# Attention and a gated product on one core: four blocks of the first product placed ahead of their Mish, one transposition by DMA, loads in another order

## The chip, the core and the metric

The kernel runs on one core of a Trainium2 chip. The core has a matrix engine (TensorE, PE in the profile; its weight loads are PEld), a vector engine (VectorE, DVE), an engine for activation functions (ScalarE, ACT), a general engine (GpSimd, POOL) and SyncE (SP), which here only issues DMA transfers. Each engine works through a queue of its own in order; semaphores join them. Matrix products go to PSUM, and VectorE or ScalarE bring them from there to SBUF. The metric is the device time of one execution in microseconds (us).

## The reference

Attention with one more term in the denominator, for 8 batches of 12 heads, 448 rows and 64 columns, and then two products with Mish between them:

```python
scores = scale * np.matmul(q, k.transpose(0, 1, 3, 2))
m = np.max(scores, axis=-1, keepdims=True)
e = np.exp(scores - m)
attn = e / (np.sum(e, axis=-1, keepdims=True) + np.exp(-m) + 1e-09)
out = np.matmul(attn, v)
...
x = out.transpose(0, 2, 1, 3).reshape(3584, 768)
h = x @ w_in                      # 768 x 2048
g = h * np.tanh(softplus(h))      # Mish
y = g @ w_out                     # 2048 x 768
```

## The kernel before

**Pairs, steps and units.** Two heads make a pair: 6 pairs per batch, 48 in all. A pair's 7 blocks of 128 score rows are handled in 4 steps, the first three with two blocks, the last with one. For each step TensorE makes the scores in one of three double PSUM tiles (`sc`), VectorE takes the negated row maximum (L293), ScalarE the exp with its sum (L306). Scores run up to three steps ahead (`scores_ahead`, L239), since a score tile is free once its exp is done.

Batch 0 (pairs 0 to 5) runs alone at the start, the head (loop at L548). Then come units of three pairs, that is 12 steps (loop at L575, `u` from 2; `n` counts steps). A unit's steps are followed by a block: the first product of half a batch (8 blocks of 128 hidden columns, 6 matmuls each, `mm1_mish`, L399), one Mish by ScalarE for each. Unit 2 and 3 hold batch 1's pairs and batch 0's first product, 4 and 5 batch 2's pairs and batch 1's first product, and so on. ScalarE loads a table when it goes from exp to Mish and another when it goes back (L649).

**Second product.** From unit 4 on, pieces of the second product fill TensorE's time between steps (`plan`, L490 and on; `mm2_part`, L443): a part is 16 matmuls for 128 rows and half of the columns (384). Unit 4 has 2.5 parts and unit 5 has 3.5, dealt out by `weight`, about a third of them at step 0.

**Normalisation, transposition, output.** After a unit's last exp the block normalises its pairs (`normalise`, L325): two by VectorE, one by GpSimd (`on_pool`), which takes a copy of the reciprocals (`rden2`) first. In the head GpSimd does four of a pair's seven blocks (`shared`). Each normalised pair has to be transposed for the output product: by a DMA that SP issues (L345), or, for the pairs in `BY_PE` (2, 4, 5, 6, 7), by four turns of TensorE of seven transposes each (L356) with a copy by VectorE (L360). `todo` (L625) sorts the unit's pairs so that those of `BY_PE` come last. `av_pair` (L368) makes the output product into a tile `mo` (there are two) and a copy `xT` (L391); from unit 4 on the output of the last unit's pair goes into the free half of the fourth step's score tile (`av_with`, L260). Copies out of `mo` are put into `late` and issued at the next `flush_late`.

**Loads.** Each pair's q, k and v (224 KB each) come by three DMAs on SP's queue, into four buffers each; GpSimd casts them to bf16 (`cast_pair`). In units this is done at steps 0, 3 and 6 (`LOAD_AT`), the load for four pairs on, the cast for three. The weights come in 20 pieces by GpSimd's queue, in order: 12 of `w_in` (256 KB, three for each quarter of its columns), 8 of `w_out` (384 KB, four for each half of its columns).

**Zeros and middle rows.** From pair 12 on, two of three pairs have their queries laid out with zero blocks (`is_diag`) so that both heads share one matmul; VectorE clears these tiles at pairs 13 and 14 (L223, L224). 448 rows are three and a half blocks of 128, so the half block of two batches is gathered in `mid` (`gather_mid`, L416).

The order of the work is written out by hand; the tables that the change touches are these:

```python
BY_PE = (2, 4, HEAD - 1, HEAD, HEAD + 1)          # HEAD = 6
AV_AT = ({3: 4, 7: 3, 9: 5}, {5: 6, 8: 7, 10: 8})   # step: pair, units 2 and 3
W_AT = ({5: 1, 9: 1}, {1: 1, 4: 1, 5: 1, 7: 1, 9: 1, 11: 1}, {3: 1, 5: 1, 7: 1, 9: 1})
```

Of the kernel before, what the change touches and what calls it, by code (L numbers as in the profile page):

```python
# [19 lines left out]
def kernel(  # L20
# [9 lines left out]
    nc = tc.nc  # L30
# [170 lines left out]
    def evac_qk(p, act=False):  # L201
        if p >= N_PAIRS:
            return
        (q_ps, k_ps), own = qkT[p]
        mo_free.extend(own)
        qd = q_diag[p % 3]
        kT = qk_pool.tile([128, S], BF16, tag="kT", name="kT")
        if not is_diag(p):
            qT = qd.rearrange("d i h r -> d (i h r)")[:, 0:S]
            qkT[p] = (qT, kT)  # L210
            if act:
                nc.scalar.mul(qT, q_ps[:, 0:S], SCALE)
            else:
                nc.vector.tensor_scalar(
                    out=qT, in0=q_ps[:, 0:S], scalar1=SCALE, scalar2=None, op0=ALU.mult
                )
            if p >= DIAG_FROM:
                nc.gpsimd.tensor_copy(out=q_rest[0:64, 0, :], in_=qT[0:64, 384:S])
                nc.gpsimd.tensor_copy(out=q_rest[64:128, 1, :], in_=qT[64:128, 0:64])
        else:  # L220
            qkT[p] = (qd, kT)
            if p < DIAG_FROM + 3:
                nc.vector.memset(qd[0:64, :, 1, :], 0.0)  # L223
                nc.vector.memset(qd[64:128, :, 0, :], 0.0)  # L224
# [100 lines left out]
    def normalise(p, dma=True, on_pool=False, shared=0):  # L325
        st = att[p]
        en = st["en"]
        if on_pool or shared:
# [3 lines left out]
        for i in range(NTILE):  # L332
# [63 lines left out]
        del att[p], casted[p], qkT[p]  # L396


    def mm1_mish(b, ff):  # L399
        if ff == 0:  # L400
            gT[b] = gT_pool.tile([128, FF_T, S], BF16, tag="gT", name="gT")
        flush_late()
        spare = ff % FF_U == 1
        h_ps = sc_tiles[0][:, 0, :] if spare else mo_take()
        for dm in range(DM_T):
            nc.tensor.matmul(  # L406
                h_ps[:, 0:S],
                lhsT=w_in_sb[:, dm, ff * 128 : (ff + 1) * 128],
                rhs=xT[b][:, dm, :],
                start=(dm == 0), stop=(dm == DM_T - 1),  # L410
            )
        nc.scalar.activation(out=gT[b][:, ff, :], in_=h_ps[:, 0:S], func=AF.Mish)  # L412
        if not spare:
            mo_free.append(h_ps)

    def gather_mid(b):  # L416
# [5 lines left out]
        nc.vector.tensor_copy(  # L422
            out=mids[g][:, :, 64 * half : 64 * half + 64], in_=gT[b][:, :, at : at + 64]
        )

# [67 lines left out]
    for g in range(B // 2):  # L493
        u0 = first_mm2 + 4 * g
        rest = plan.pop(u0, [])
        if g == 0:
            plan[u0] = [(0, i, 0, 2) for i in range(2)] + [(0, 2, 0, 1)]
            plan[u0 + 1] = [(0, 2, 1, 1)] + [(0, i, 2, 2) for i in range(3)]
        else:
            plan[u0] = rest + whole(g, 0) + [(g, 1, 0, 1)]  # L500
            plan[u0 + 1] = [(g, 1, 1, 1), (g, 1, 2, 2)] + whole(g, 2)
# [4 lines left out]
        else:  # L506
# [5 lines left out]
    BY_POOL = 4  # L512
    LEAD = UNIT_PAIRS + 1
    LOAD_AT = (0, 3, 6)
    LAST_AV_AT = (0, 6, 9)
    HEAD = HP

    BY_PE = (2, 4, HEAD - 1, HEAD, HEAD + 1)
    TURN_AT = (
        {0: [(4, 2)], 1: [(4, 3)], **{3 + j: [(HEAD - 1, j)] for j in range(NT)}},  # L520
        {0: [(HEAD, 0), (HEAD, 1)], 1: [(HEAD, 2)], 2: [(HEAD, 3)],
         3: [(HEAD + 1, 0)], 4: [(HEAD + 1, 1)], 5: [(HEAD + 1, 2)], 6: [(HEAD + 1, 3)]},
    )
    TURN_HEAD = {
        (3, 2): [(2, 0)], (3, 3): [(2, 1)], (4, 0): [(2, 2)], (4, 1): [(2, 3)],
# [49 lines left out]
    for u in range(UNITS_PER_B, N_UNITS + 2 * UNITS_PER_B):  # L575
# [3 lines left out]
            filler.extend(mm2_part(*part))  # L579
        total, done, acc = sum(w for _, w in filler), 0, 0.0  # L580
        p0 = u * UNIT_PAIRS
        if attn and u >= first_mm2:
            av_with.update({p0 + i: p0 + i - UNIT_PAIRS for i in range(UNIT_PAIRS)})
        end = min((u + 1) * UNIT_PAIRS, N_PAIRS) * STEPS

        for n in range(steps):
# [18 lines left out]
            scores_ahead(end)  # L605
            if n in LOAD_AT:
                load_pair(p0 + LOAD_AT.index(n) + LEAD)
                cast_pair(p0 + LOAD_AT.index(n) + LEAD - 1)
            if u - UNITS_PER_B < len(AV_AT):
                early = AV_AT[u - UNITS_PER_B]  # L610
                if n in early:
                    av_pair(early[n])
                if u == UNITS_PER_B:
# [33 lines left out]
        if attn and u + 1 < N_UNITS:  # L647

            nc.scalar.activation(out=one, in_=zero, func=AF.Exp)  # L649
        if moe and w == UNITS_PER_B - 1:  # L650
            gather_mid(b)
    flush_late()
    assert not pieces and all(have == 4 for _, have in o_sbs.values())
# [30 lines left out]
```

## Time and profile before

| | us |
|---|---|
| median of three runs | 480.3 (480.15 to 481.88) |
| the profiled execution | 479.95 |
| its span, first to last instruction | 478.0 |
| TensorE busy in it | 443.1 (93%) |
| ScalarE busy | 350.0 (73%) |
| VectorE busy | 339.1 (71%) |
| GpSimd busy | 181.1 (38%) |

The first exp of unit 3 starts at 76.75, that of unit 4 at 104.29, of unit 5 at 130.17, of unit 6 at 156.91. A line of the page names a place in the code (L406), an engine, an operation, and tiles (`gT<-mo`). A digit in a row of 40 is a busy share in tenths. Start-to-start times are the ones to use for matmuls, since one begins while the last still runs: an L406 block of six takes 1.14 us, a matmul of 384 columns at L472 0.163 us. The granted clock of TensorE is 1.00 or 0.50 in stretches of 3.41 us; it was 0.50 at 44.5 to 54.8, 78.7 to 82.1 and 88.9 to 92.3 of the span.

### The profile page before, as it was taken

What the parts mean: (1) busy time and instruction counts of PE and PEld (TensorE: products, weight loads), DVE (VectorE), ACT (ScalarE), POOL (GpSimd) and SP (SyncE); (2) the same over time, 40 slices, a digit from 0 to 9 for tenths busy, and PEclk for the clock granted to TensorE, in tenths of its full rate; (3) what the DMA queues carried; (4) which work ended last, traced back from release to release, by engine and by line L of the source; (5) the groups of instructions that cost most, each with busy time, mean ns of one, the idle gap of its engine ahead of it and who ended that gap; (6) DMA issues with size and microseconds to landing.
All of it is one profiled execution on the core that took longest, in us unless ns stands there. A gap on an engine that the chain in (4) does not pass through costs nothing.

```text
span 478.0 us, 8924 instructions
## 1 busy us (share of the span) xinstructions
PE 443.1 (93%) x3064; PEld 248.6 (52%) x3064; DVE 339.1 (71%) x680; ACT 350.0 (73%) x919; POOL 181.1 (38%) x315
## 2 busy tenths in 40 slices
PE   4565888898999999999999999999999999999997
PEld 2233544454655555555555555556555555556565
DVE  4888987968787886878687878788787869420021
ACT  5979678878787888979787878888897978412300
POOL 4877809255514334353535242433535340300000
PEclk9998798899999999999999999999999999999999
DMA  8999969999999989899999999899989595870113
GB/s 228 220 233 220 235 100 234 162 187 238 207 217 276 206 212 219 213 203 246 193 250 182 225 167 228 211 207 234 201 233 212 156 178 127 135 164 24 43 28 105
DMA packets 202381, 90.37 MB, mean 189 GB/s; under 512 B 159072, under 2 KB 198880, under 8 KB 202336
## 3 DMA queue, kind: packets, MB, share of 16 engines
q1 hardware_dynamic: 194848, 83.51, 81.3%
q0 software_dynamic: 7488, 6.29, 8.6%
q8 instruction: 24, 0.39, 0.3%
q14 instruction: 21, 0.17, 0.1%
HBM read 45.61 MB, written 11.01 MB: 118 GB/s over the span
## 4 chain that ended last, share of the span: by engine, by line
PE 76%; ACT 10%; DVE 9%; issue 2%; DMA 1%; POOL 0%; SPq 0%; DVEq 0%; ACTq 0%; POOLq 0%
PE mo L472 26%; PE mo L406 25%; ACT en L306 9%; PE sc L382 6%; DVE negm L293 6%; PE sc L266 5%; PE sc L406 4%; PE sc L193 3%; PE sc L272 2%; PE mo L356 1%; PE mo L382 1%; DVE en L341 1%; PE sc L280 1%; DVE eT L360 1%; DMA k_f<-in_k_dram 1%
## 5 line engine op out<-in xcount | busy, mean ns | idle before, releaser
L306 ACT ACTIVATE en<-sc,negm 128x448 bf16<-128x448 f32 x336 | 209.6, 637 | 26.4 <-DVE xT L391 10.4
L293 DVE TENSOR_REDUCE negm<-sc 128x2 f32<-128x896 f32 x192 | 180.7, 968 | 55.8 <-PE sc L275 26.0
L472 PE MATMUL mo<-w_out_sb,gT 128*128 128x384 bf16 (+1 forms) x912 | 142.3, 301 | 0.0
L406 PE MATMUL mo<-xT,w_in_sb 128*128 128x448 bf16 x672 | 137.7, 353 | 0.6 <-DVE xT L391 0.6
L412 ACT ACTIVATE gT<-mo 128x448 bf16<-128x448 f32 x112 | 61.3, 547 | 68.2 <-PE mo L406 68.1
L472 PEld LDWEIGHTS <-gT 128*128 128x128 bf16 x912 | 84.1, 98 | 48.2 <-issue 5.7
L339 POOL TENSOR_SCALAR en<-en,rden 128x448 bf16<-128x448 bf16 x122 | 76.4, 646 | 80.7 <-DVE rden L331 76.9
L406 PEld LDWEIGHTS <-w_in_sb 128*128 128x128 bf16 x768 | 72.9, 98 | 64.0 <-issue 3.0
L306 ACT ACTIVATION_READ_ACCUMULATOR en<-sc,negm 128x1 f32 x336 | 69.3, 206 | 0.0
L175 POOL CAST q_bf<-q_f 112x512 bf16<-112x512 f32 x47 | 29.0, 617 | 98.4 <-DMA q_f<-in_q_dram 98.0
L341 DVE TENSOR_SCALAR en<-en,rden 128x448 bf16<-128x448 bf16 x214 | 58.6, 345 | 0.9
L459 DVE COPY o_sb<-mo 128x384 f32<-128x384 f32 (+1 forms) x65 | 32.2, 495 | 35.1 <-PE mo L472 34.8
L266 PE MATMUL sc<-kT,qd 128*128 128x448 bf16 x168 | 47.7, 354 | 0.3 <-ACT en L306 0.2
L272 PE MATMUL sc<-kT,qd 64*128 64x448 bf16 x72 | 25.1, 411 | 12.7 <-ACT en L306 11.1
L382 PE MATMUL sc<-eT,v_bf 112*64 112x448 bf16 x288 | 34.1, 357 | 1.9 <-ACT en L306 1.7
L162 POOL CAST v_bf<-v_f 112x512 bf16<-112x512 f32 x48 | 29.5, 616 | 9.7 <-DMA v_f<-in_v_dram 8.8
L382 PEld LDWEIGHTS <-v_bf 112*64 112x64 bf16 x384 | 21.0, 112 | 22.8 <-issue 13.6
L176 POOL CAST k_bf<-k_f 112x512 bf16<-112x512 f32 x47 | 28.9, 616 | 7.5 <-DMA k_f<-in_k_dram 7.0
L227 DVE TENSOR_SCALAR qd<-sc 64x448 bf16<-64x448 bf16 x48 | 18.7, 389 | 11.9 <-PE sc L193 11.2
L266 PEld LDWEIGHTS <-qd 128*128 128x128 bf16 x168 | 16.3, 97 | 18.0 <-issue 9.2
L275 PE MATMUL sc<-kT,qd 64*128 64x448 bf16 x72 | 25.4, 415 | 0.0
L472 PE MATMUL mo<-w_out_sb,mid 128*128 128x384 bf16 x128 | 24.9, 326 | 0.0
(57 smaller groups left out, 340.1 us busy)
## 6 DMA issues: line engine op xcount, KB each, us to landing
q_f<-in_q_dram SPq DMA_DIRECT2D x48, 224.0 KB, 5.1
k_f<-in_k_dram SPq DMA_DIRECT2D x48, 224.0 KB, 5.4
v_f<-in_v_dram SPq DMA_DIRECT2D x48, 224.0 KB, 5.7
w_in_sb<-in_moe_w_in_dram POOLq DMA_DIRECT2D x12, 256.0 KB, 6.1
w_out_sb<-in_moe_w_out_dram POOLq DMA_DIRECT2D x8, 384.0 KB, 7.6
out_dram<-o_sb SPq DMA_DIRECT2D x7, 336.0 KB, 3.3
out_dram<-o_sb SPq DMA_DIRECT2D x8, 288.0 KB, 4.6
out_dram<-o_sb SPq DMA_DIRECT2D x8, 240.0 KB, 2.9
```

Of the source, the lines that this page charges most:

```text
L162: nc.gpsimd.tensor_copy(out=casted[p][2], in_=loaded.pop(p)[2])
L266: nc.tensor.matmul(sc[:, bk, 0:S], lhsT=qT[:, i].rearrange("d h r -> d (h r)"), rhs=kT, start=True, stop=True,)
L272: nc.tensor.matmul(sc[:, 0, 0:S], lhsT=qT[0:64, qa : qa + 128], rhs=kA, start=True, stop=True)
L293: nc.vector.tensor_reduce(out=negm, in_=sc[:, 0 : len(cols), 0:S], axis=AX.X, op=ALU.max, negate=True)
L306: nc.scalar.activation(out=st["en"][:, :, c, 0:SP_], in_=sc[:, bk, 0:S].rearrange("q (j c) -> q j c", j=NT), func=AF.Exp, bias=st["negm"][ ...
L339: nc.gpsimd.tensor_scalar(scalar2=1.0, op0=ALU.mult, op1=ALU.mult, **args)
L341: nc.vector.tensor_scalar(scalar2=None, op0=ALU.mult, **args)
L382: nc.tensor.matmul(av[h * 64 : (h + 1) * 64, 0:S], lhsT=v_bf[:, h, j * D : (j + 1) * D], rhs=e_h, start=(j == 0), stop=(j == NT - 1),)
L406: nc.tensor.matmul(h_ps[:, 0:S], lhsT=w_in_sb[:, dm, ff * 128 : (ff + 1) * 128], rhs=xT[b][:, dm, :], start=(dm == 0), stop=(dm == DM_T - 1),)
L412: nc.scalar.activation(out=gT[b][:, ff, :], in_=h_ps[:, 0:S], func=AF.Mish)
L459: nc.vector.tensor_copy(out=o_sb[:, cols], in_=st["o"][:, 0:n_cols])
L472: nc.tensor.matmul(st["o"][:, 0:n_cols], lhsT=src[:, ff, c0 : c0 + 128], rhs=w_out_sb[:, ff, cols], start=(ff == 0), stop=(ff == FF_T - 1),)
```

## The change

- **First product ahead.** In unit 3, four of batch 0's blocks (8 to 11) are multiplied at steps 5, 7, 9 and 10, each into an `mo` tile, and copied by VectorE to an `o_sb` buffer in float32. In the block their Mish reads that buffer. Blocks 12 to 15 stay in the block; the two kinds alternate (`SECOND`). The block that uses a score tile (`spare`) is now the second of each unit's list.
- **Seventh pair.** Pair 6 leaves `BY_PE`; unit 2 normalises 6, 8 (VectorE), 7 (GpSimd), and two DMA transpositions are issued there. Pair 7's turns on TensorE are at steps 1 to 4 of unit 3; the outputs of pairs 6, 7, 8 at steps 3, 6, 8.
- **Loads.** Pairs 13 and 14 are loaded in unit 2 (step 9, block), 15, 16 and 17 in unit 3 (steps 0 and 10, block), 18 in unit 4's block. Casts stay where they are.
- **Weights.** In unit 2's block two pieces are issued at its third place instead of one each at the third and seventh; unit 3 issues its six by step 9 instead of 11; unit 4 three at steps 4 and 5 and the last in its block, instead of four up to step 9.
- **Unit 4 and 5.** Outputs of pairs 9, 10, 11 are made at steps 3, 7, 10 of unit 4 into `mo` tiles; `av_with` starts with unit 5. The second product has 3 parts in each of the two units.
- **GpSimd.** It clears the zero blocks once, ahead of unit 3's block, and gathers batch 0's half block at step 8 of unit 5.
- **Head.** For pairs 0 and 1 VectorE's three normalisations come ahead of the `rden2` copy and GpSimd's four.

```diff
-            if p < DIAG_FROM + 3:
-                nc.vector.memset(qd[0:64, :, 1, :], 0.0)
-                nc.vector.memset(qd[64:128, :, 0, :], 0.0)
...
+        order = list(range(NTILE))
+        if shared and p < 2:
+            order = order[shared:] + order[:shared]
+        for i in order:
+            if i == 0 and (on_pool or shared):
+                for_pool()
...
+    def mm1_ahead(b, ff):
+        h_ps = mo_take()
+        mm1(b, ff, h_ps)
+        h_sb = o_pool.tile([128, d_model], FP32, tag="o_sb", name="o_sb")
+        h_sbs[b, ff] = h_sb
+        def evac():
+            nc.vector.tensor_copy(out=h_sb[:, 0:S], in_=h_ps[:, 0:S])
+            mo_free.append(h_ps)
+        late.append(evac)
+
+    def mm1_mish(b, ff, spare):
...
+        if (b, ff) in h_sbs:
+            nc.scalar.activation(out=gT[b][:, ff, :], in_=h_sbs.pop((b, ff))[:, 0:S], func=AF.Mish)
+            return
...
-            plan[u0] = [(0, i, 0, 2) for i in range(2)] + [(0, 2, 0, 1)]
-            plan[u0 + 1] = [(0, 2, 1, 1)] + [(0, i, 2, 2) for i in range(3)]
+            plan[u0] = [(0, i, 0, 2) for i in range(3)]
+            plan[u0 + 1] = [(0, i, 2, 2) for i in range(3)]
...
+    W_MISH = {(2, 2): 2, (4, 1): 1}
+    LOADS = {
+        2: ({0: 10, 3: 11, 6: 12, 9: 13}, {1: 14}),
+        3: ({0: 15, 10: 16}, {4: 17}),
+        4: ({}, {1: 18}),
+    }
...
-    BY_PE = (2, 4, HEAD - 1, HEAD, HEAD + 1)
+    BY_PE = (2, 4, HEAD - 1, HEAD + 1)
     TURN_AT = (
...
-        {0: [(HEAD, 0), (HEAD, 1)], 1: [(HEAD, 2)], 2: [(HEAD, 3)],
-         3: [(HEAD + 1, 0)], 4: [(HEAD + 1, 1)], 5: [(HEAD + 1, 2)], 6: [(HEAD + 1, 3)]},
+        {1 + j: [(HEAD + 1, j)] for j in range(NT)},
...
-    AV_AT = ({3: 4, 7: 3, 9: 5}, {5: 6, 8: 7, 10: 8})
-
-    W_AT = ({5: 1, 9: 1}, {1: 1, 4: 1, 5: 1, 7: 1, 9: 1, 11: 1}, {3: 1, 5: 1, 7: 1, 9: 1})
+    AV_AT = ({3: 4, 7: 3, 9: 5}, {3: 6, 6: 7, 8: 8}, {3: 9, 7: 10, 10: 11})
+    FIRST_AT = {5: FF_U, 7: FF_U + 1, 9: FF_U + 2, 10: FF_U + 3}
+    SECOND = [ff for i in range(4) for ff in (FF_U + i, FF_U + 4 + i)]
+
+    W_AT = ({5: 1, 9: 1}, {1: 1, 2: 1, 4: 1, 5: 1, 7: 1, 9: 1}, {4: 2, 5: 1})
...
-        if attn and u >= first_mm2:
+        if attn and u > first_mm2:
...
+            if (u, n) == (first_mm2 + 1, 8):
+                gather_mid(0, nc.gpsimd.tensor_copy)
...
+        if u == UNITS_PER_B + 1:
+            for t_ in q_diag[1:]:
+                nc.gpsimd.memset(t_[0:64, :, 1, :], 0.0)
+                nc.gpsimd.memset(t_[64:128, :, 0, :], 0.0)
...
-                mm1_mish(b, w * FF_U + f)
-            if u == UNITS_PER_B and f in (2, 6):
-                load_w(1)
+                mm1_mish(b, SECOND[f] if u == UNITS_PER_B + 1 else w * FF_U + f, spare=f == 1)
```

More of the change, by code (lines that the diff above doesn't have):

```diff
@@ L327, in normalise, with for_pool @@
         en = st["en"]
-        if on_pool or shared:
+        def for_pool():
             st["rden2"] = st_pool.tile([128, NTILE], FP32, tag="rden2", name="rden2")
             nc.vector.tensor_copy(out=st["rden2"], in_=st["rden"])
-        for i in range(NTILE):
+        order = list(range(NTILE))
[4 more added lines that the diff above has]
+                for_pool()
             pool_does = on_pool or i < shared
@@ L396, in av_pair, with mm1 @@
         del att[p], casted[p], qkT[p]
[L399 to L404, printed above, removed]
+    def mm1(b, ff, h_ps):
         for dm in range(DM_T):
@@ L411, in mm1_mish @@
             )
+    h_sbs = {}
+    def mm1_ahead(b, ff):
[8 more added lines that the diff above has]
+    def mm1_mish(b, ff, spare):
+        if ff == 0:
+            gT[b] = gT_pool.tile([128, FF_T, S], BF16, tag="gT", name="gT")
+        flush_late()
+        if (b, ff) in h_sbs:
+            nc.scalar.activation(out=gT[b][:, ff, :], in_=h_sbs.pop((b, ff))[:, 0:S], func=AF.Mish)
+            return
+        h_ps = sc_tiles[0][:, 0, :] if spare else mo_take()
+        mm1(b, ff, h_ps)
         nc.scalar.activation(out=gT[b][:, ff, :], in_=h_ps[:, 0:S], func=AF.Mish)
@@ L414, in mm1_mish, with gather_mid @@
             mo_free.append(h_ps)
-    def gather_mid(b):
+    def gather_mid(b, copy=nc.vector.tensor_copy):
         g, half = divmod(b, 2)
@@ L421, in gather_mid @@
         at = S - 64 if half == 0 else 0
-        nc.vector.tensor_copy(
+        copy(
             out=mids[g][:, :, 64 * half : 64 * half + 64], in_=gT[b][:, :, at : at + 64]
@@ L605 @@
             scores_ahead(end)
+            if u in LOADS:
+                if n in LOADS[u][0]:
+                    load_pair(LOADS[u][0][n])
+            elif n in LOAD_AT:
+                load_pair(p0 + LOAD_AT.index(n) + LEAD)
             if n in LOAD_AT:
-                load_pair(p0 + LOAD_AT.index(n) + LEAD)
                 cast_pair(p0 + LOAD_AT.index(n) + LEAD - 1)
@@ L612 @@
                     av_pair(early[n])
+                if u == UNITS_PER_B + 1 and n in FIRST_AT:
+                    mm1_ahead(0, FIRST_AT[n])
                 if u == UNITS_PER_B:
@@ L627 @@
             if moe:
-                mm1_mish(b, w * FF_U + f)
-            if u == UNITS_PER_B and f in (2, 6):
-                load_w(1)
+                mm1_mish(b, SECOND[f] if u == UNITS_PER_B + 1 else w * FF_U + f, spare=f == 1)
+            if (u, f) in W_MISH:
+                load_w(W_MISH[u, f])
+            if u in LOADS and f in LOADS[u][1]:
+                load_pair(LOADS[u][1][f])
             if not attn:
@@ L649 @@
             nc.scalar.activation(out=one, in_=zero, func=AF.Exp)
-        if moe and w == UNITS_PER_B - 1:
+        if moe and w == UNITS_PER_B - 1 and b > 0:
             gather_mid(b)
```

## The prediction

> **What bounds the kernel now.** I read first the 40 slices of the page, to see where TensorE stops being the bound.
>
> ```profile
> PE   4565888898999999999999999999999999999997
> ...
> ACT  5979678878787888979787878888897978412300
> ...
> PEclk9998798899999999999999999999999999999999
> ```
>
> From the eleventh slice (119.5 us) on TensorE is full nearly to the end, so work taken off it there, or moved ahead of there, is worth its length; before, it has holes. The table by stretches shows the holes. I cut at ScalarE's first and last exp of units 2 to 5, so the rows alternate between steps and product block.
>
> ```profile
> 76.75:91.90 15.15, 11.62 (x86) 6.71 (x86) 12.97 (x19) 13.44 (x43) 9.94 (x16) 0.79 1.16 208
> 91.90:104.30 12.40, 12.40 (x87) 6.75 (x86) 8.98 (x29) 8.60 (x18) 4.65 (x9) 0.98 0.90 160
> 104.30:119.30 15.00, 13.07 (x89) 7.22 (x88) 12.76 (x18) 13.56 (x44) 7.83 (x14) 1.00 1.08 228
> ...
> 130.20:145.30 15.10, 15.08 (x96) 7.85 (x95) 12.50 (x18) 13.62 (x43) 3.70 (x7) 1.00 1.05 228
> ```
>
> Columns: length, then busy time of PE, PEld, DVE, ACT, POOL, granted clock, DMA share, GB/s. In unit 3's steps (76.75 to 91.90) TensorE has 3.5 us free and ScalarE is the pace (13.4 of 15.2). In its block (91.90 to 104.30) it is the other way round: PE 12.4 of 12.4, ScalarE only 8.6. The chain of waits says what ends that block:
>
> ```profile
> 91.48 1.67 PE mo L406 x6
> 93.16 1.13 PE sc L406 x6
> ...
> 94.68 2.27 PE mo L406 x12
> ...
> 97.35 2.27 PE mo L406 x12
> ...
> 100.02 2.29 PE mo L406 x12
> ...
> 102.89 1.28 ACT L649
> ```
>
> All eight blocks of L406 stand on it one after another, 1.14 us each, then the table load that lets unit 4's exps begin at 104.29.
>
> **The change, part by part.**
>
> *Four blocks of the first product move from unit 3's block into its steps.* 24 matmuls leave a stretch where PE is the bound: 4 x 1.14 = 4.55 us. What bounds it then? ScalarE: it ends the steps at 92.15 (expm), then loads a table (1.28), does 8 Mish and 3 kT copies and loads again (1.28 + 0.20). Where these stand back to back they start 0.43 apart (unit 2's block, 66.29, 66.73, 67.15), so 92.17 + 1.28 + 11 x 0.43 + 1.28 + 0.20 = 99.7. VectorE: den and rden to 92.7, 7 normalisations 1.81, q 0.39, q 0.79, 7 normalisations 1.81, rden copy 0.17, q 0.79, first reduction 1.08: 99.55. PE: 4 x 1.14 + 3 transposed pairs x 0.40 + first scores = 6.1, slack of 1.5 to 2. So 104.3 becomes 99.7: **-4.6** if the steps end as before.
>
> *What the steps pay for it.* PE there: 24 matmuls come (4.55), 28 transposes of the seventh pair go (4 x 0.60 to 0.99, half of them ahead of 78 in a hole). VectorE: four copies of 448 floats to SBUF come (0.55 to 0.61, by the o_sb rows of 384: 0.55), four eT copies (0.61) go. That is even in sum, not in place: two of those that go ran at 76.09, where VectorE then stood idle 1.37 us, and the new ones lie in the chain score, reduction, exp. Before the last reduction VectorE now has 8 copies, before 7: **+0.5**. At the end of the steps three results wait for two PSUM tiles (pair 8's output, then blocks of steps 9 and 10): the last block can't start before pair 8's output is copied, so some 91.9 to 93.0, and its copy ends by 93.6, ahead of den on VectorE's queue. That is up to 1.3 more; a step of two exps lasts 1.23 and a block 1.14, so I take 0.3 of it. Sum: -4.6 + 0.5 + 0.3 = **-3.8** (from -4.6 to -2.8).
>
> *Seventh pair by DMA.* Its transposition is issued at 67.4, in place of pair 8's, which took 4.2 us of SP and 7.9 to land: 75.3, against an output product at step 3 (80.5). Pair 8's goes behind it and load 14 (three issues, 1.5): 71.6 + 1.5 to 77.4, landed by about 81, wanted at step 8 (86). DMA had nothing at all to do from 64 to 67.4. Cover is 5 us for each: nothing. Without it PE would stand at that output product, with the next scores behind it in its queue.
>
> *Loads.* 13 goes to unit 2's step 9 (its buffer is free when pair 9's cast ends, 54), 14 into the block behind pair 6's transposition, 15 and 16 into unit 3's steps, 17 between pair 10's and 11's transpositions, 18 into unit 4's block between pair 12's and 13's. Today 16 to 18 come behind three transpositions at 108.8 and POOL waits 5.9 us for a cast; that wait goes and was covered (its q is transposed at 122.5). Price: SP issues 17 (1.5 us) ahead of pair 11's transposition, which waits for POOL's normalisation anyway; its 672 KB at some 230 GB/s take 2.9 us. Pair 11 lands today at 110.7, then at worst 114; the change wants it at step 10 of unit 4 (112 to 113) instead of step 8, and the block's first matmul at 114. Nothing to +1. Load 18 likewise delays pairs 13 and 14 by 1.5 to 4, but w_out's pieces (1.5 MB, issued today at 115 to 120, when pair 13's issue took 7.2 us) are then out of the way: even.
>
> *w_in and w_out pieces.* The ninth and tenth pieces go ahead of POOL's normalisation (72.2), to about 58 to 61, so blocks 8 to 11 have their weights 20 us early; pieces of blocks 12 to 15 come at steps 1 and 2. Nothing.
>
> *Zeros and the first gather to POOL.* Four DVE memsets leave the block (4 x 0.245 = 1.0, already left out of my VectorE sum) and one copy of 0.78 leaves unit 4's step 0. POOL has no memset of that shape: bounds 0.20 (ident, 128x128 bf16) and 0.62 (a cast of 512), so 0.8 to 2.5 for four; they wait for pair 11's last scores (88.6) and end by 91.1 at worst, wanted at 95. The gather on POOL, twice a cast, some 1.2, is wanted two units later. One row speaks against POOL's help: seven normalisations took 2.97 beside POOL's casts (146.09) and 1.81 alone. The Trainium skill ("SBUF — State Buffer", Who interferes with whom) says why: VectorE's fast modes and GpSimd take one port pair, and the other is blocked wholly. By that rule memsets that slip into the block would cost their length, up to 2.5; by the times above they don't meet a normalisation.
>
> *Fifth unit.* Outputs of pairs 9 to 11 go from steps 0, 4, 8 to 3, 7, 10, and in PSUM tiles of their own; today 0.95 of matmuls stands between step 0's exps and the next score, and ScalarE loses 1.5 us to VectorE in unit 4. The second product's plan moves half a part (8 x 0.163 = 1.3) from unit 5, where PE has no hole (15.08 of 15.10), to unit 4, which has 1.9. Unit 5 can't get below unit 4's pace of ScalarE, so of 1.3 I count 0.3, and 0.2 for the gather and the order: **-0.3** with AV 11's risk taken in, from -1.5 to +1.
>
> *Pairs 0 and 1 normalised on VectorE first.* POOL starts 0.75 later (17.65 to 18.4), its casts with it; pair 4's k cast then ends at 22.3 and its transpose began at 22.21: +0.1; VectorE's three run without POOL beside them (0.82 against 1.13): -0.2. **0**, +-0.3.
>
> **Sum.** -3.8 - 0.3 = -4.1 on an execution of 479.95 (span 478.0 and 1.95 around it): 475.85. The median of the runs is 480.3, 0.35 above it: **476.2**.
>
> **Rivals.**
>
> *The clock takes half of it back.* Granted clock by windows:
>
> ```profile
> 75.26:78.67 3.41, 1.25 (x19) 1.00 0.89 257
> 78.67:82.08 3.41, 3.29 (x25) 0.50 1.04 234
> 82.08:85.50 3.42, 2.92 (x30) 1.00 1.18 183
> 85.50:88.90 3.40, 1.87 (x20) 1.00 1.27 192
> 88.90:92.30 3.40, 3.40 (x19) 0.50 1.31 202
> ```
>
> After windows with 1.25 and 1.87 us of PE the next ran at half, after 2.92 at full. In the new block PE has 6.1 of 8, about 2.6 per window: between the two. One half window takes 1.7 us of PE work; the slack is 1.5 to 2, but the block's Mish wait for those matmuls in turn. Price 1 to 2.5: **478.2**. The Trainium skill ("TensorE: Matmul & The Clock Gate", HAM oscillation) asks only that no idle gap exceeds about 3.4 us. By that rule this rival has no price; the rows disagree, since here the longest gap before a half window was 2.2.
>
> *Slower, by the same gate.* If unit 3's steps and block stay at half: steps hold 12.4 us of PE work at full clock (9 scores 2.6, 4 turns 2.4, 3 outputs 2.85, 4 blocks 4.55), so 2.8 are free. Each half window costs 1.7; the one at 78.67 stays and leaves 1.1. Five more, all from 82 to 99, cost 8.5 - 1.1 = 7.4: **483.6**. From four on (5.7) the gain of 4.1 is gone. Against: a window at half is a full one (3.29, 3.40), and full clock followed each time.
>
> *No change.* The pace of the steps swallows it: VectorE 14.0 busy of 15.2 with each copy ahead of a reduction, PE's block behind each score; if every block delays a reduction by its own 1.14, 4.1 of gain goes: **480.3**. For: ScalarE waited 0.71 for scores at 86.87 behind an output and a turn in one step. Against: the others did not.
>
> *More.* The block at its floor (-4.6), steps not longer, units 4 and 5 at -1.5: **474.2**.
>
> **How the numbers follow.** Forecast 0.55, half given back 0.19, no change 0.08, slower 0.08, more 0.10. About 0.5% (2.4 us) is what a measurement of this kernel can tell from no change. Faster by more than that, below 477.9: 0.55 x 0.95 + 0.10 + 0.19 x 0.45 = 0.71, within 0.21, slower 0.08. The range leaves out the slower case and half of no change and of the best end: 473.9 to 479.8.
>
> **What would show it.** Unit 3's block 8 to 8.5 us from last exp to first, with ScalarE back to back in it; unit 3's steps 15 to 16; eight L406 blocks split four and four; units 4 and 5 together 52 to 53; full clock from 82 on. Wrong: steps above 17, a half window inside the block, or a wait of PE for eT in unit 4.

## The result and the profile after

The changed kernel took **494.67 us** (median of four runs, 493.64 to 496.09) against 480.23 (479.39 to 481.88) for the kernel before on the same chip: a ratio of **1.0294 [1.0273, 1.0315]**. It is slower by 14.4 us where 4 us of gain were forecast. The profiled execution has a span of 493.0, 15.0 over the 478.0 of before.

The 40 slices (each now 12.3 us long) show one place at once:

```profile
PE   4476897992598999999999999999999999999997
...
ACT  5979678894078787878888797979787878603300
...
PEclk9998797997599999999999999999999999999999
...
GB/s 234 209 227 245 252 144 218 194 203 115 82 208 259 200 212 182 232 217 227 207 204 231 221 181 205 240 189 260 170 262 178 194 163 153 110 184 1 64 17 112
```

In the tenth and eleventh slice (111 to 136 us) TensorE is busy 2 and 5 tenths, ScalarE 4 and 0, the granted clock is 7 and 5 tenths, and the DMA engines move 115 and 82 GB/s where the slices around have some 200. The table by stretches, cut as before at ScalarE's first and last exp of units 3 to 5:

```profile
76.97:92.65 15.68, 13.97 (x89) 6.85 (x89) 12.79 (x18) 13.63 (x43) 11.12 (x19) 0.78 1.16 225
92.65:102.37 9.72, 8.83 (x67) 4.84 (x66) 8.45 (x26) 8.55 (x17) 2.38 (x6) 1.00 1.08 160
102.37:115.90 13.53, 11.89 (x73) 5.83 (x70) 11.89 (x15) 13.05 (x43) 10.51 (x17) 1.00 1.14 167
115.90:145.20 29.30, 15.80 (x97) 7.91 (x98) 8.83 (x26) 8.59 (x17) 4.55 (x9) 0.71 0.92 135
145.20:160.40 15.20, 13.86 (x88) 7.29 (x87) 12.41 (x17) 13.50 (x43) 4.47 (x9) 1.00 1.05 253
```

Columns: length, then busy time of PE, PEld, DVE, ACT, POOL, granted clock, DMA share, GB/s. Unit 3's steps are 15.68 (15.15 before), its block 9.72 (12.40), unit 4's steps 13.53 (15.00): up to 115.9 the changed kernel is 3.4 us ahead. Then unit 4's block takes 29.30 us instead of some 10.9 (119.30 to 130.20), and from there on every unit has the length that it had. The chain of waits, with start and length of each piece, crosses that block so:

```profile
93.91 0.62 DVE o_sb L421
94.53 0.10 DVE den L316
...
107.38 0.51 DMA v_f<-in_v_dram
107.89 21.47 DMA eT<-en
...
129.40 1.71 PE mo L385 x8
```

The last column is the engine, tile and line of a piece. One piece takes 21.47 us: the DMA transposition of pair 11, issued by SP at 107.89, landed at 129.36. The page's chain has it as "DMA eT<-en 4%", which the page of before does not list. The waits say who stood:

```profile
ACT gT L435 <- PE mo L404: 81.9, 81, 16.7
...
PEld L385 <- DMA eT<-en: 15.5, 1, 15.5
PE mo L385 <- DMA eT<-en: 15.1, 1, 15.1
```

Columns: engine, result and line, what it waited for, the sum, how often, the longest. TensorE stood 15.1 us in one piece, ahead of pair 11's output product, with all of unit 4's block queued behind it; ScalarE's Mish waited 16.7 for that block, its longest. In the kernel before the same transposition took 6.2 us (104.5 to 110.7).

What lengthened it is on the other queue. GpSimd's instructions in this stretch, first before, then after (start, length, the idle time ahead and what ended it):

```profile
112.06 0.62 POOL L175 CAST q_bf<-q_f 112x512 bf16<-112x512 f32 x1 [5.93 <-DMA q_f<-in_q_dram]
...
115.09 1.55 POOL L158 DMA_DIRECT2D w_out_sb<-in_moe_w_out_dram  x2
...
118.30 1.48 POOL L158 DMA_DIRECT2D w_out_sb<-in_moe_w_out_dram  x2
```
```profile
106.43 0.61 POOL L175 CAST q_bf<-q_f 112x512 bf16<-112x512 f32 x1
...
108.10 2.30 POOL L158 DMA_DIRECT2D w_out_sb<-in_moe_w_out_dram  x3
...
112.86 0.75 POOL L158 DMA_DIRECT2D w_out_sb<-in_moe_w_out_dram  x1
```
```profile
96.86 9.29 SPq L348 DMA_TRANSPOSE eT<-en  x2
106.24 0.53 SPq L132 DMA_DIRECT2D q_f<-in_q_dram  x1
...
107.89 10.72 SPq L348 DMA_TRANSPOSE eT<-en  x1
```

Before, GpSimd stood 5.93 us for the load of pair 16 (112.06), and its last four pieces of `w_out` were issued at 115.09 and 118.30, when pair 11's transposition had landed. After, the loads are early, nothing holds GpSimd, and three pieces go out at 108.10, 0.2 us behind the issue of the transposition (third fence). That transposition is itself issued 3.4 us later than before: the row of transpositions on SP starts 1.8 us later (96.86, before 95.03), and the three issues of load 17 take 1.65; that load's packets then go ahead of its own. Both then want the same DMA engines. The packet counts by queue, first for three microseconds of pair 11's transposition before, then for three of it after:

```profile
q1 hardware_dynamic: 2536, 0.65, 114.9%
...
eT<-en SPq DMA_TRANSPOSE x1, 6.2
```
```profile
q0 software_dynamic: 491, 0.37, 90.4%
q1 hardware_dynamic: 485, 0.12, 41.8%
```

Columns: packets, MB, share of the 16 engines; the line of the transposition ends with its time from issue to landing. Queue q1 carries what SP issues, q0 the pieces of GpSimd. Alone, the transposition moves 2536 packets in 3 us (845 per us); beside the pieces 485, that is 162 per us, one for each of their 491. A packet of the transposition, 256 bytes, occupies an engine 22 ns when alone (1.149 x 16 x 3 us / 2536); one of a piece, some 750 bytes, takes 88 ns here (0.904 x 48 us / 491). So there the pieces, 1.5 MB in all, set the pace of a tile that the output product waits for. At the start of the collision turns of one for one don't explain the pace: from 114 to 118 the transposition was as slow, 170 packets per us, beside only 54 of the pieces (last section). The Trainium skill ("DMA: Bandwidth & Descriptors", Issuing engines are not separate DMA queues) says that DMAs run on the same 16 engines and interleave, whichever engine issued them. The counts agree. From 120 to 123 they are equal by packets, not by bytes, so the queue with the short packets loses most there.

### The profile page after: what moved, and what is told of

It reads as the page before. It is cut to its first block, busy times and chain, and to the rows that moved or that the text cites. A ratio compares the mean times of both kernels' runs of the same rounds, so it can differ in the third digit from the quotient of the medians.

```text
span 493.0 us, 8836 instructions
## 1 busy us (share of the span) xinstructions
PE 443.9 (90%) x3020; PEld 245.7 (50%) x3020; DVE 337.2 (68%) x674; ACT 349.8 (71%) x919; POOL 183.3 (37%) x320
## 4 chain that ended last, share of the span: by engine, by line
PE 73%; ACT 9%; DVE 8%; DMA 5%; issue 2%; POOL 1%; SPq 0%; DVEq 0%; ACTq 0%
PE mo L495 25%; PE mo L404 25%; ACT en L303 7%; PE sc L385 5%; DVE negm L290 5%; PE sc L263 5%; DMA eT<-en 4%; PE sc L404 3%; PE sc L193 3%; PE sc L269 3%; PE mo L385 2%; PE mo L359 1%; DVE en L344 1%; POOL en L342 1%; PE mo L193 1%
## 5 line engine op out<-in xcount | busy, mean ns | idle before, releaser
L435 ACT ACTIVATE gT<-mo 128x448 bf16<-128x448 f32 x108 | 59.1, 547 | 82.2 <-PE mo L404 81.9
L495 PEld LDWEIGHTS <-gT 128*128 128x128 bf16 x896 | 82.7, 98 | 49.9 <-issue 7.2
L269 PE MATMUL sc<-kT,qd 64*128 64x448 bf16 x72 | 25.7, 414 | 13.0 <-ACT en L303 11.2
L385 PE MATMUL sc<-eT,v_bf 112*64 112x448 bf16 x264 | 31.3, 357 | 1.6 <-ACT en L303 1.3
L385 PE MATMUL mo<-eT,v_bf 112*64 112x448 bf16 x120 | 17.0, 414 | 15.9 <-DMA eT<-en 15.1
L224 DVE TENSOR_SCALAR qd<-sc 64x448 bf16<-64x448 bf16 x48 | 18.7, 389 | 12.1 <-PE sc L193 11.4
L272 PE MATMUL sc<-kT,qd 64*128 64x448 bf16 x72 | 26.0, 419 | 0.0
```

Of the source, the lines that this page charges most:

```text
L269: nc.tensor.matmul(sc[:, 0, 0:S], lhsT=qT[0:64, qa : qa + 128], rhs=kA, start=True, stop=True)
L385: nc.tensor.matmul(av[h * 64 : (h + 1) * 64, 0:S], lhsT=v_bf[:, h, j * D : (j + 1) * D], rhs=e_h, start=(j == 0), stop=(j == NT - 1),)
L495: nc.tensor.matmul(st["o"][:, 0:n_cols], lhsT=src[:, ff, c0 : c0 + 128], rhs=w_out_sb[:, ff, cols], start=(ff == 0), stop=(ff == FF_T - 1),)
```

## The experiments

The theory at the start (A): the pieces of `w_out` beside pair 11's transposition cost the 15 us, and they are there because the earlier loads took GpSimd's wait away. Rivals: load 17 ahead of that transposition alone (B); a loss in unit 4 itself, by outputs in other tiles and copies ahead of reductions (C). The price of the first product's four blocks is tested further on (D). Ratios are to the kernel before, run on the same chip; times of units are from one profile of each kernel. Diffs are against the changed kernel unless they say otherwise. Where a quoted text defines letters of its own, they hold for that experiment.

**The loads back in their old places.**

```diff
-    LOADS = {
-        2: ({0: 10, 3: 11, 6: 12, 9: 13}, {1: 14}), ...
+    LOADS = {}
```

> The changed kernel with the table of loads emptied: pairs 13 to 18 are loaded where they were before the change; all else stays. Theory A (mixture): pair 11's transposition takes 21.5 us to land because w_out's last four pieces are in flight with it; they got there since GpSimd no longer waits for the casts of pairs 16 and 17. With the loads back GpSimd waits again, the pieces are issued some 7 us after the transposition, it lands in 6 to 7 us, and the time is 474 to 478. Theory B (order on SP): pair 11's transposition is late because load 17 stands ahead of it; undone here too, so the same time, but the pieces may then be anywhere. Theory C (the loss lies in unit 4 itself: outputs in mid-block tiles, copies ahead of reductions): 488 to 494.

Measured: 485.03, ratio 1.0095 [1.0066, 1.0125]. Pair 11's transposition took 6.1 again (landed 112.5) and the 15 us are gone, as A has it; but the time forecast was missed. The pieces went out at 116.68, though the steps at which the changed program has them stayed: it was the loads that had brought them early. They now met pair **12's**: 12.9 us instead of 9.3. That is the same collision a place further on, ScalarE in unit 5 behind it:

```profile
ACT en L303 <- DVE xT L394: 5.2, 2, 5.1
```

**The loads early, the last pieces held to unit 4's block.**

```diff
-    W_MISH = {(2, 2): 2, (4, 1): 1}
+    W_MISH = {(2, 2): 2, (4, 2): 4}
-    W_AT = (..., {4: 2, 5: 1})
+    W_AT = (..., {})
```

> The changed kernel with w_out's last four pieces moved out of unit 4's steps to the third place of its block, where GpSimd comes only after the copies of q_rest; load 17 stays ahead of pair 11's transposition. Theory A: pair 11's transposition lands in 6 to 9 us and unit 4 has no wait for it; pair 12's, issued at about the same time as the pieces, takes 14 to 20 us instead, and what unit 5 waits for it is up to 6 us: 478 to 486. Theory B: load 17 still stands ahead of pair 11's transposition, so it still lands 15 us late: 490 to 495. Theory C: 488 to 494, without a wait for a transposition.

Measured: 490.55, ratio 1.0207 [1.0177, 1.0237]. Pair 11's transposition, with load 17 still ahead of it, took 7.7: load 17 alone (B) does not make the stall. The time lies in the range that B and C had (490 to 495, 488 to 494) and above A's 478 to 486, but for another reason than theirs. The pieces, issued at 120.94, met pairs 12 and 13 (11.1 and 15.0 us), and were themselves too late: TensorE waited 7.8 us for `w_out`, ScalarE 11.7 behind outputs.

**The kernel before, with its pieces issued early and nothing else.** Against the kernel before:

```diff
-    W_AT = (..., {3: 1, 5: 1, 7: 1, 9: 1})
+    W_AT = (..., {})
...
+            if u == UNITS_PER_B + 1 and f == 2:
+                load_w(4)
```

> The kernel before with one thing changed: w_out's last four pieces are issued at the third place of unit 3's block (about 96 us), beside the transpositions of pairs 9 and 10, instead of at 115 to 120 us. Theory A: pair 9's transposition, alone 6.2 us, takes 14 to 20 us, unit 4 waits 6 to 10 us for it, and the time is 486 to 492. If pieces only stand in line ahead of a transposition (1.5 MB at 200 GB/s, 7.7 us at most, split over two transpositions): 480 to 484. Theories B and C say nothing of this kernel but that it stays at 480.

Measured: 484.33, ratio 1.0083 [1.0051, 1.0114]. None of the change is in this kernel but the collision, and it is slower. Transpositions of pairs 9 and 10 took 11.1 and 15.1 us (before 6.2 and 6.1), unit 4's steps 22.2 instead of 16.5 between table loads. The direction and the mechanism are as A has them; the price was smaller than forecast: 4.0 us between the medians (484.33 and 480.34). The profiled execution, the slowest of the four, has a span 5.7 us longer, all of it in unit 4's steps. Five microseconds of pair 10's:

```profile
q0 software_dynamic: 953, 0.72, 91.4%
q1 hardware_dynamic: 953, 0.24, 37.0%
```

953 packets each: one for one, at 191 per us.

**Three loads back behind the transpositions.**

```diff
-        3: ({0: 15, 10: 16}, {4: 17}),
-        4: ({}, {1: 18}),
+        3: ({0: 15}, {}),
+        4: ({0: 16, 3: 17, 6: 18}, {}),
```

> The changed kernel with only pairs 16, 17 and 18 loaded where they were before (unit 4's steps); 13, 14 and 15 stay sooner. Theory A: as with all loads back, since it is the cast of pair 16 that holds the pieces: 474 to 478. Were the sooner loads of 13 to 15 of use, it would be below the kernel with all loads back; by the profile they are not, so within 0.5 us of it. Theory C: 488 to 494.

Measured: 484.36, ratio 1.0094 [1.0059, 1.0128]. As with all loads back: pair 11's 6.1, pieces at 116.61, pair 12's 12.6, unit 5's steps 21.2 between table loads instead of 16.8. The forecast of 474 to 478 was missed for the same reason.

**A gate.** GpSimd reads one column of pair 11's transposed tile at step 4 of unit 4, ahead of the pieces, so these can't start before the transposition has landed.

```diff
+    gate = singles.tile([128, 1], BF16)
...
+            if (u, n) == (first_mm2, 4):
+                nc.gpsimd.tensor_copy(out=gate, in_=att[p0 - 1]["eT"][:, 0, 0:1])
```

> The changed kernel with one thing added: at step 4 of unit 4 GpSimd copies one element of pair 11's transposed tile, so that w_out's last three pieces (and the fourth) are issued only when that transposition has landed. Theory A: it lands in 7 to 8 us (some 115.6), unit 4's block begins at 115 to 116 and the wait of 15 us is gone; the pieces are then on the DMA engines at 117 to 127, beside pair 12's transposition (issued near 120), which takes 10 to 13 us instead of 6, as with the loads back: 483 to 487. Theory D (the four blocks ahead and the copies that go with them cost more than they bring): the time is the same but pair 12's transposition lands in 6 to 7 us.

Measured: 484.55 (483.05 to 488.81), ratio 1.010 [1.0046, 1.0155]. Pair 11's took 7.6 and TensorE waited 1.1 us for it instead of 15.1.

```profile
117.99 0.19 POOL L658 COPY gate<-eT 128x1 bf16<-128x1 bf16 x1 [7.32 <-DMA eT<-en]
118.22 2.29 POOL L159 DMA_DIRECT2D w_out_sb<-in_moe_w_out_dram  x3
```

Load 17, the outputs and the four blocks are all as in the changed kernel, so neither B alone nor C makes the 15 us. The four pieces, issued at 118.22 and 122.29, met pair 12's (10.6). The profiled execution is the slowest of these runs, with a start (to unit 3) 2.6 us longer than the changed kernel's, so its later times say little.

**The gate, with fewer pieces left behind it.** Two more pieces go out in unit 2's block, one less in unit 3's steps and none in unit 4's block, so three are left behind the gate.

```diff
-    W_MISH = {(2, 2): 2, (4, 1): 1}
+    W_MISH = {(2, 2): 4}
-    W_AT = ({5: 1, 9: 1}, {1: 1, 2: 1, 4: 1, 5: 1, 7: 1, 9: 1}, {4: 2, 5: 1})
+    W_AT = ({5: 1, 9: 1}, {1: 1, 2: 1, 4: 1, 5: 1, 7: 1}, {4: 2, 5: 1})
```

> As the run before, and the pieces spread over stretches in which no transposition is in flight: four instead of two at the third place of unit 2's block (DMA idle at 64 to 68), five in unit 3's steps, the last three after pair 11's landing. Theory A: every transposition of units 2 to 5 lands in 6 to 9 us, no wait for one above 1 us, and the whole of the gain at unit 4's first exp (1.9 us) and unit 4's steps (1.1) comes through: 475.5 to 478. Theory D: 482 or more though no transposition is late.

Measured over ten runs: 480.95 (478.14 to 482.49), ratio 1.0006 [0.9986, 1.0026]. Pair 11's took 7.2, pair 12's 8.3, less than the 9.3 of before. With the collision out of the way the kernel is as fast as the one before, not faster: the forecast of 475.5 to 478 was missed by 3 us, and D's 482 or more did not come either.

**The same, and the four blocks a step earlier** (so that fewer results wait for the two PSUM tiles at the end of unit 3's steps).

```diff
-    FIRST_AT = {5: FF_U, 7: FF_U + 1, 9: FF_U + 2, 10: FF_U + 3}
+    FIRST_AT = {4: FF_U, 5: FF_U + 1, 7: FF_U + 2, 9: FF_U + 3}
```

> As the run before, with the four blocks ahead at steps 4, 5, 7 and 9 instead of 5, 7, 9 and 10. VectorE's first instruction of unit 3's block (den) then no longer waits for the last block's copy (in the changed kernel den begins at 94.45, 1.5 us after ScalarE's last instruction): unit 3's block gets 1 to 1.5 us shorter, 474 to 477. If steps 4 and 5 delay scores instead, it is as the run before or up to 1 us slower.

Measured over ten runs: 480.83, ratio 1.0011 [0.9988, 1.0034]. Unit 3's block got shorter (6.9 between table loads, 8.0 in the changed kernel, 10.7 before), its steps longer (17.9, 17.4, 16.8). The forecast of 474 to 477 was missed. The gain arrived at unit 4's start and was lost at its block:

```profile
116.00 0.95 PE L386 MATMUL mo<-eT,v_bf 112*64 112x448 bf16 x8 [1.34 <-DMA eT<-en]
...
117.67 1.29 PE L405 MATMUL mo<-xT,w_in_sb 128*128 128x448 bf16 x6 [0.29 <-DVE xT L395]
```

Start, length, engine, line, and the idle time ahead. TensorE waits for pair 11's transposition (landed 116.0), and the block's first matmul starts at 117.67, where the kernel before has it at 117.73. What it waits for is a row on SP's queue: pair 9's, pair 10's, load 17, pair 11's.

**The first product ahead, alone, in the kernel before** (`mm1_ahead`, `FIRST_AT` and `SECOND` of the change, nothing else of it).

> The kernel before with one part of the change alone: four blocks of batch 0's first product at steps 5, 7, 9 and 10 of unit 3, and the alternation in its block. Loads, weights, transpositions and outputs stay. Unit 4's exps begin 1.5 to 2.5 us sooner. Theory A: loads 16 to 18 and so the pieces come as much sooner as pair 12's transposition does, so its landing stays near 9 to 11 us and the gain comes through: 477.5 to 480. Theory D: 480.5 or more.

Measured: 483.65, ratio 1.0066 [1.004, 1.0093]. Unit 3's block is 2 us shorter and its steps 1.2 longer, but units 4 and 5 have steps of 18.2 and 18.5 instead of 16.5 and 16.8 between table loads. With outputs still at steps 0, 4 and 8, and transpositions that start some 3 us later (pair 11's lands at 114.0), ScalarE stands behind outputs and PE behind transpositions:

```profile
ACT en L306 <- DVE xT L391: 5.0, 6, 1.7
...
PE sc L382 <- DMA eT<-en: 1.7, 2, 0.9
```

So the first part of the change, with the outputs where they were, costs 3 us instead of bringing 4, as D has it (480.5 or more), but makes no 15 us stall.

**Load 17 behind pair 11's transposition.** Three kernels with one edit in common: in the first it is added to the gate, the pieces spread and the blocks a step earlier, in the second it is alone, in the third it is added to the gate and the pieces spread.

```diff
-        3: ({0: 15, 10: 16}, {4: 17}),
-        4: ({}, {1: 18}),
+        3: ({0: 15, 10: 16}, {}),
+        4: ({0: 17}, {1: 18}),
```

> The pieces wait for pair 10's transposition and are issued one at a time, the first product's four blocks go a step earlier, and load 17 is moved from ahead of pair 11's transposition to behind it. Theory A (what is left after the mixture is taken away is the row of transpositions on SP: pair 9, pair 10, load 17, pair 11, then pair 11's output, then unit 4's block): pair 11's transposition starts at about 106.6 instead of 108.3 and lands at 112 to 114 instead of 116.0, unit 4's block gives back 2 to 3 us, time 477.5 to 479.5. Theory B (the row does not bound unit 4's block; PE's own work there does): the transposition lands sooner and the block keeps its 12 us between table loads, time 480 to 482. Theory C (load 17, now later, makes pair 17's casts on POOL late and gives the time back in unit 5): transposition sooner, unit 5's first exp later than in the same kernel with the load ahead.

> The changed kernel with load 17 alone moved behind pair 11's transposition; the pieces of w_out stay where they are (three issued at about 108, packets from about 112). Theory A (the stall needs both: pieces sooner and the transposition 1.5 us later): pair 11's packets run from about 106.5 to 112 and are nearly through when the pieces' packets begin; it lands at 112 to 115, the 15 us wait of PE is gone, time 478 to 483. Theory B (the pieces alone are enough): it lands at 120 or later, time 485 or more.

> As the first kernel of this call, but with the first product's four blocks in the changed kernel's own steps (5, 7, 9, 10). Theory A: the row of transpositions starts where the changed kernel has it, pair 11's lands at 112.5 to 114.5 and the time is 478 to 480; the order one step earlier is worth less than 1 us either way. Theory B: 480 to 482, as with the load ahead.

(In the first text the gate is said to wait for pair 10's; it is pair 11's, as in all kernels with the gate.)

Measured, the second first: **482.54** (479.95 to 484.32), ratio 1.0023 [0.9998, 1.0047]. One edit takes 12 of the 14.4 us away. The pieces went out at 107.05 (this execution is 1.0 us ahead from unit 3's block on), but pair 11's transposition was issued at 105.2, 1.9 us ahead of them instead of 0.2, with no load before it:

```profile
q1 hardware_dynamic: 3151, 0.80, 109.8%
```
```profile
q0 software_dynamic: 536, 0.40, 130.6%
```
```profile
PE mo L385 <- DMA eT<-en: 2.3, 1, 2.3
```

The first fence is 106 to 110, the second 112 to 114. From 106 to 110 SP's queue has the engines to itself, and by 111.6 all the packets of 256 bytes are through; the first pieces' packets came at 111, four microseconds behind their issue. In the second window there are 536 packets of pieces and none of SP's queue. Some 30 small packets (under 512 bytes each) came from 114.2 to 115.2; I take them to be those that close the transposition, which landed at 115.5, 10.3 us from its issue. PE waited 2.3 us instead of 15.1. So the stall needed both, the pieces sooner and the transposition later; neither was enough alone (load 17 ahead and the pieces later: 7.7 us).

The first: **479.10** over twelve runs (477.6 to 481.23), ratio 0.998 [0.9963, 0.9997]; the third 479.92, ratio 0.9985 [0.9969, 1.0001]. Pair 11's landed at 112.8, 3.2 sooner than with the load ahead:

```profile
112.83 0.19 POOL L658 COPY gate<-eT 128x1 bf16<-128x1 bf16 x1 [4.28 <-DMA eT<-en]
113.07 2.31 POOL L159 DMA_DIRECT2D w_out_sb<-in_moe_w_out_dram  x3
```
```profile
101.40:116.60 15.20, 14.72 (x91) 7.29 (x91) 14.19 (x19) 14.71 (x45) 10.82 (x19) 1.00 1.10 219
116.60:127.30 10.70, 10.70 (x78) 5.79 (x76) 6.37 (x24) 6.92 (x13) 3.75 (x8) 1.00 1.22 201
```

The windows are cut at table loads (unit 4's steps, unit 4's block; before 16.5 and 9.3). The row on SP bounded unit 4's block, as A has it, but for less than the 2 to 3 us forecast: it gives 1.4 back (10.7 instead of 12.1), and 1.0 in the third kernel (10.7, with the load ahead 11.7). C, time given back in unit 5, is not clear: against the same kernel with the load ahead, unit 5's block is 0.8 longer in the first (10.5 and 9.7) and 0.5 shorter in the third (10.6 and 11.1), its steps are equal. Steps and block of unit 4 together still take 26.0 us, 25.9 before, with TensorE busy 14.72 and 10.70 in them. The change moved half a part of the second product there, so B, TensorE's own work, was tried last.

**The half part of the second product back in unit 5.** Added to the first of these three:

```diff
-            plan[u0] = [(0, i, 0, 2) for i in range(3)]
-            plan[u0 + 1] = [(0, i, 2, 2) for i in range(3)]
+            plan[u0] = [(0, i, 0, 2) for i in range(2)] + [(0, 2, 0, 1)]
+            plan[u0 + 1] = [(0, 2, 1, 1)] + [(0, i, 2, 2) for i in range(3)]
```

> The fastest kernel so far (gate, pieces spread, blocks a step earlier, load 17 behind pair 11's transposition), with the half part of the second product (8 matmuls, 1.3 us) put back from unit 4 into unit 5, as in the kernel before. Theory A (TensorE is the bound in unit 4, busy 25.4 of 25.9 us there, and free in unit 5's steps, 15.56 of 16.90): unit 4's steps and block get 0.8 to 1.3 shorter, from 25.9 to about 24.9, unit 5's steps stay at 16.9, and the time is 477.8 to 478.7. Theory B (unit 5's steps have no use for the free time, since it lies where TensorE waits for exps): unit 4 gets shorter, unit 5's steps longer by as much, 479 to 480. Theory C (unit 4 is bound by pair 11's transposition or VectorE after all): unit 4 as long as before, 479 to 480.5.

Measured: 479.67 over twelve runs (478.87 to 481.53), ratio 0.9987 [0.9973, 1.0001]; no gain over 479.10. A falls: with 1.4 us less for TensorE in its steps, unit 4's steps and block took 26.6. The time fits B and C, but B's longer steps in unit 5 did not come (16.7), and pair 11's transposition landed at 111.5, ahead of its use, so C's first half is out as well.

```profile
99.80:115.00 15.20, 13.28 (x89) 7.06 (x89) 13.68 (x18) 14.96 (x46) 10.71 (x19) 1.00 1.10 220
115.00:126.40 11.40, 11.12 (x80) 5.98 (x77) 6.93 (x25) 6.95 (x13) 3.88 (x9) 1.00 1.19 219
```
```profile
113.74 0.95 PE L386 MATMUL mo<-eT,v_bf 112*64 112x448 bf16 x8
...
115.41 1.29 PE L405 MATMUL mo<-xT,w_in_sb 128*128 128x448 bf16 x6 [0.28 <-DVE xT L395]
```

In the steps ScalarE is now the pace (14.96 of 15.20) and TensorE has 1.9 us free; in the block TensorE goes through 8 products, three transposed pairs and the next scores one behind the other, 11 us from 115.41. It starts there because pair 11's output product stands at step 10 (113.74) and all 8 products read its copy `xT`. In the kernel before, with that output at step 8, the first product began 1.7 us ahead of the table load (117.73 against 119.44), here 0.4 behind (115.41 against 115.03). So the later outputs, which the shorter steps need, put 2.1 us back into the block. That is read from these lines; no run moved pair 11's output alone. Of the 2.3 us that this execution is ahead at unit 5's start (126.4 against 128.8), 0.7 are left in the span; units 5 to 7 lost 0.3 or 0.4 each and the units behind them the rest, for which no cause was found.

The kernel with the load behind, 479.10, has the lowest median, a fifth of a per cent under the kernel before; from 479.92 and 479.67 it can't be told apart, since the runs of each spread over some 3 us.

## Why the prediction was wrong

**Where it failed.** The step called "Loads". It said of GpSimd's 5.9 us wait "that wait goes and was covered", put pair 11's transposition at "at worst 114", gave the whole "Nothing to +1", and held the pieces of `w_out` to be "then out of the way: even". The wait was not idle cover: it was what kept 1.5 MB of pieces off the DMA engines until the transposition had landed. The prediction counted the packets of load 17 ahead of that transposition and asked when POOL's casts would be late; it did not ask what POOL would issue next, and sooner, once it no longer waited. Measured: 129.4 instead of 114, 15.1 us of TensorE. Even with the pieces held back it would have landed at some 115.6 (issued at 107.86 and 7.7 us long in the second experiment), so the worst case was too early as well. Its last sentence named "a wait of PE for eT in unit 4" as what would make it wrong, without a rival that had it.

**By its other steps.**

- *Four blocks, -4.6.* This was mis-sized, with the two terms below. Eight blocks were split four and four, and ScalarE went back to back in places only. Unit 4's first exp came at 102.37, where the sum had 100.5 (99.7 with 0.8 for the steps and the tiles): a gain of 1.9, not 3.8.
- *Steps, +0.5.* The table load at their end is at 92.95, before at 92.17: +0.8, close.
- *Two PSUM tiles, 0.3 of up to 1.3.* This term was mis-sized. The last copy out of `mo` began at 93.91 (the chain above), and `den` behind it at 94.53, where the sum had about 92.2: 2.3 later, of which 0.8 are the steps. So 1.5, over the upper bound. The prediction had the row that tells it ("its copy ends by 93.6, ahead of den on VectorE's queue") and priced it by a step's slack instead.
- *Fifth unit, -0.3.* Unit 4's steps were 13.5 instead of 15.0, better than that, but the block behind them gave 1.4 back even without the stall. The outputs were costed as a small gain by themselves. With them left in place, the four blocks made the steps of units 4 and 5 some 1.7 us longer each.
- *Seventh pair by DMA, w_in pieces, zeros, gather, head: nothing.* The profile shows no stall by them; they were not tried one by one.

**The rivals.** The clock did not take half back: in the new block (92.30 to 102.53) it was full.

```profile
82.08:85.50 3.42, 3.42 (x23) 1.69 (x21) 2.94 (x4) 3.05 (x10) 3.42 (x7) 0.50 1.09 245
...
95.71:99.12 3.41, 2.80 (x28) 1.72 (x27) 2.92 (x12) 2.59 (x6) 0.47 (x2) 1.00 1.04 82
99.12:102.53 3.41, 3.13 (x22) 1.44 (x19) 3.33 (x10) 3.31 (x7) 2.07 (x4) 1.00 0.92 207
```

The half clock at 116.7 to 133.8 came behind the start of the stall (114.3) and was no cause of it:

```profile
128.00:132.00 4.00, 2.60 (x11) 0.94 (x12) 0.72 (x2) 0.00 (x0) 0.00 (x0) 0.50 0.36 54
132.00:136.00 4.00, 4.00 (x23) 2.01 (x22) 3.04 (x11) 1.27 (x3) 0.00 (x0) 0.77 0.02 5
```

From pair 11's output product to the table load it took 14.4 us, and 12.7 both in the kernel of the seventh experiment and in the one with load 17 behind, which leaves some 1.7 us to the clock. The 18.3 us that the block grew are then, as an estimate from three kernels, 15.1 of stall, 1.7 of clock, and 1.4 that it is longer without either (10.7, measured in the kernel with load 17 behind, against 9.3). Unit 3's steps had the half clock for about two windows, as before, in another place (82.08, the first row). The slower rival (483.6, by the clock) had the right sign for a wrong reason. "No change" came true once the collision was taken out (480.95 and 480.83), but by another way than its own, which was the pace of unit 3's steps: behind each gain stood a next bound, first SP's row of transpositions, then, as read from the trace, the place of pair 11's output.

**The sum as measured**, between table loads, after against before: start +0.2, unit 3's steps +0.6, its block -2.7, unit 4's steps -1.3, its block +18.3, unit 5 0.0: 15.1, and 15.0 in the span.

## What to carry to other kernels

When a change takes an engine's wait away, look up what that engine issues next: a wait of GpSimd for a load was here what kept its weight pieces from meeting a transposition that TensorE needed. Moving loads earlier on one queue moves the DMAs of another, so draw the packets of all queues on one time axis, and give a tile that somebody waits for an idle DMA stretch or a real dependency for its rival to wait on. And before a stretch is counted as gain, look for the next thing that everything behind it reads: here pair 11's copy, first by its DMA, then by its place in the steps.

## What the runs showed of the hardware

- Packets of GpSimd's pieces (converted to bf16 on the way) and of a DMA transposition went one for one on the DMA engines where both queues were full: 953 and 953 in 5 us (the kernel before with its pieces early), 491 and 485 in 3 (the changed kernel). The transposition fell from 845 packets per us to 191 and 162, and its time from 6.2 us to 15.1 and 21.5.
- At the start of the collision it was worse than turns explain. From 114 to 118 the changed kernel's engines were full with 682 packets of the transposition, 93 ns each (0.988 x 16 x 4 us / 682; 22 alone), and 217 of the pieces, 140 ns each (78 alone: 1.306 x 32 us / 536). In the kernel before with its pieces early the first kind took 31 ns and the second 77. Why they took three times and nearly twice as long here stays open; so the collision's price in the changed kernel is explained in part only.

```profile
q1 hardware_dynamic: 682, 0.17, 98.8%
q0 software_dynamic: 217, 0.16, 47.3%
```

- The first packets of a piece came between 1.5 and 5 us behind its issue by GpSimd: 4 us in the kernel with load 17 alone behind (107.05 and 111), under 2 with the gate and load 17 behind (113.07 and 114.6 to 115.1), 2.5 to 3 in the changed kernel, over 4.5 in the kernel before with its pieces early. The Trainium skill ("DMA: Bandwidth & Descriptors", Latency and other measured facts) gives about 1 us to the first byte on this path; the traces show more, and they decide.
- The end of a transposition can lag its data: with pieces under way its last packet of 256 bytes came by 111.6, no packet of SP's queue followed until 114.2, and it landed at 115.5.
